# First row tile of q's weights in two transfers, second token half on the other queue, first products in halves

## The chip, the cores and the metric

The kernel runs on one core of one Trainium2 chip. The metric is the device time of one execution in microseconds (us), as the median of several runs. In this kernel TensorE's matmuls are what the profile calls PE, its weight loads PEld; ScalarE is ACT, VectorE DVE, GpSimd POOL, SyncE SP. SP and ACT issue the transfers (DMAs), each on a queue of its own.

## The reference

One layer with two branches on the same 2048 tokens of width 448, mixed by a gate for each token:

```python
x = A_x                                          # (1, 2048, 448)
g = sigmoid((x * gate_w).sum(-1, keepdims=True))
qkv = x @ wqkv                                   # (448, 3*448); 16 heads of 28
# each query looks at 8 keys, its own position and those 2, 4 .. 14 before it
a = (softmax(q . k[pos - 2*w] * 28**-0.5) @ v) @ wo
h = x @ w1 + b1                                  # (448, 1792)
b = relu(h)**2 @ w2 + b2
return g * a + (1 - g) * b
```

All of it is float32.

## The kernel before, in words

Every matrix product is made of three: each operand is split into a high part (a rounded copy, made by ACT or DVE: wqh, x.h, w1h ...) and a low part (the rest, subtracted by DVE: wql, x.l, w1l ...), and PE adds high x high, high x low and low x high in PSUM. A split starts from a raw tile that a transfer brings in from memory (wqraw, xraw).

The 448 rows of a contraction are three row tiles of 128 (k = 0, 1, 2) and one of 64 (k = 3). The tokens are four chunks of 512 (x0 to x3), a chunk four tiles of 128 tokens. For each chunk PE makes q, k and v; then the MLP's h and its output b follow for all chunks, with the attention beside it on POOL and DVE, and the product with wo (a) at the end. q's weights carry two more columns with the gate's weights, so q's products are 450 columns wide, k's and v's 448. The columns are streamed in a woven order: the first of the left half, the first of the right half, the second of the left half, and so on. In the weights' tile the two halves lie apart: 225 columns, one free, 225 columns.

Two things set the order of the work. At the start it is the order in which the code is written: scratch products on zeros (L816, WARM of them, 256 columns each), the first transfers (L819 to L838), and the splits of the first chunk and of q's weights (L839 to L858). Then a planner (class Plan) takes over: it holds a modelled time for PE, starts at START, adds each product's cost, and lets ACT, DVE, POOL and SP issue their jobs in the order in which they would come due. START and FIRST, the modelled length of the first three stretches of products, thus decide where later casts, evacuations and transfers stand.

The first real products are those of qkv_first (L430): four accumulators q[0] to q[3], one for each token tile, in four PSUM banks. For k = 0 it takes the tiles (0, 1), then (2, 3), since the tokens' first half (256 tokens, two tiles) is brought and cast before the second; within a pair the order is high x high, high tokens x low weights, low tokens x high weights. For k = 1 and 2 all four tiles go together. These are the products of L439. From k = 3 on, products of 64 rows run in pairs side by side (L351).

The first transfers: SP issues weights and tokens in turn, 128 rows each; ACT issues the two halves of the first tokens (L823). A transfer's completion is counted on one of eight semaphores that all queues share in turn, so SP's ninth transfer or so waits for the first ones to land. For k = 0 the weights' left half is cast by ACT (L846), the right half by DVE (L847), then DVE casts the tokens' first half (L848) and subtracts the low parts (L850, L854); ACT casts the second half of the tokens (L853).

## Time and profile before

| | before |
|---|---|
| runs (us) | 392.57, 392.83, 392.65; median 392.65 |
| profiled execution: span, first to last instruction | 391.0 us (the page gives its time as this span; the runs' median is 1.65 above it) |
| PE busy | 386.5 us, 99% of the span |
| DVE, POOL, ACT busy | 261.4, 260.6, 205.4 us |
| first scratch product / first real product starts | 0.79 / 5.01 us |
| first product of 64 rows starts | 12.35 us |
| granted TensorE clock over the span | 1.000 |

The profile is one execution. Its page gives the busy time of each engine, the chain of work that ended last, and groups of instructions; its timeline gives rows in the order of time with start and length in us, engine and line, output<-inputs, shape and count, and in brackets how long the engine was idle before and what ended that. A q behind an engine's name is its sequencer, which issues transfers. A matmul's length in a row includes the time until its result has left the array, so rows that follow each other overlap; the distance between starts is the pace.

### The profile page before, as it was taken

The page shows a single profiled execution, that of the slowest core. Times are in us where ns is not written, and L with a number is a line of the kernel's source. Part 1 is how long each engine was busy: PE and PEld are TensorE (multiplying, and loading weights), DVE is VectorE, ACT ScalarE, POOL GpSimd, SP SyncE. Part 2 cuts the span into 40 slices and gives each one's busy share as a digit, 9 for nine tenths or more (in the row PEclk, how much of TensorE's full clock was granted, in tenths as well). Part 3 has the DMA queues.
Part 4 walks back from the last instruction along what each step waited for, and adds up shares of the span by engine and source line. Part 5 has one row for each costly group of instructions (what it writes and reads, how often), then busy time and mean ns, then how long its engine had stood idle before and what let it go on. Part 6 is the DMA issues. An engine that isn't in the chain of part 4 may idle for free.

```text
span 391.0 us, 9273 instructions
## 1 busy us (share of the span) xinstructions
PE 386.5 (99%) x3828; PEld 385.2 (99%) x3828; DVE 261.4 (67%) x348; ACT 205.4 (53%) x501; POOL 260.6 (67%) x165
## 2 busy tenths in 40 slices
PE   9999999999999999999999999999999999999996
PEld 8999999999999999999999999999999999999995
DVE  4525523588685778778656989789666686668454
ACT  4757866362566566445555445345716343456740
POOL 0000002988999989959999887999998979661000
PEclk9999999999999999999999999999999999999999
DMA  7999999997174062654203779655635120226835
GB/s 236 400 355 302 382 376 350 378 370 246 49 246 157 1 219 80 220 171 161 90 2 137 242 183 296 208 124 141 213 111 173 78 96 2 88 63 164 143 107 188
DMA packets 64841, 73.75 MB, mean 189 GB/s; under 512 B 32480, under 2 KB 57632, under 8 KB 64416
## 3 DMA queue, kind: packets, MB, share of 16 engines
q1 hardware_dynamic: 64368, 72.79, 57.2%
q8 instruction: 30, 0.49, 0.5%
q10 hardware_dynamic: 432, 0.38, 0.3%
q14 instruction: 11, 0.09, 0.1%
HBM read 45.71 MB, written 28.25 MB: 189 GB/s over the span
## 4 chain that ended last, share of the span: by engine, by line
PE 99%; DVE 0%; DVEq 0%; issue 0%
PE b L351 33%; PE h L351 32%; PE qkv L351 23%; PE a L351 7%; PE qkv L439 2%; PE warm L817 1%; PE a L1170 1%; DVE bt_b L1053 0%; DVEq L1375 0%
## 5 line engine op out<-in xcount | busy, mean ns | idle before, releaser
L549 POOL TENSOR_TENSOR pp<-q,k 128x896 f32<-128x896 f32 x56 | 116.9, 2124 | 75.1 <-DMA k<-k_d 64.4
L561 POOL TENSOR_TENSOR pp<-lg,v 128x896 f32<-128x896 f32 x64 | 113.8, 1870 | 9.6 <-DVE o L571 5.3
L351 PE MATMUL h<-x,w1h 64*128 64x512 f32 x672 | 116.6, 376 | 0.0
L351 PE MATMUL qkv<-wqh,x 64*128 64x448 f32 (+1 forms) x528 | 82.2, 349 | 0.0
L553 DVE TENSOR_REDUCE lg<-pp 128x32 f32<-128x896 f32 x64 | 66.9, 1076 | 13.9 <-POOL pp L549 13.9
L351 PEld LDWEIGHTS h<-x,w1h 64*128 64x128 f32 x672 | 74.1, 186 | 0.0
L803 DVE TENSOR_TENSOR h<-h,h 128x512 fp32r<-128x512 f32 x56 | 38.6, 690 | 52.4 <-ACT h L802 52.3
L351 PE MATMUL h<-x,w1l 64*128 64x512 f32 x336 | 69.3, 376 | 0.0
L351 PE MATMUL b<-w2bh,h 64*128 64x448 f32 x448 | 67.8, 349 | 0.0
L351 PE MATMUL b<-w2ah,h 64*128 64x448 f32 x448 | 67.6, 349 | 0.0
L571 DVE TENSOR_REDUCE o<-pp 128x112 f32<-128x896 f32 x64 | 67.4, 1064 | 0.0
L351 PEld LDWEIGHTS qkv<-wqh,x 64*128 64x128 f32 x528 | 57.3, 186 | 0.0
L799 ACT ACTIVATE h<-h,b1z 128x512 f32<-128x512 f32 x56 | 36.7, 655 | 36.8 <-PE h L351 36.8
L351 PE MATMUL qkv<-wql,x 64*128 64x448 f32 (+1 forms) x264 | 53.4, 349 | 0.0
L351 PEld LDWEIGHTS b<-w2bh,h 64*128 64x128 f32 x448 | 48.0, 192 | 0.0
L351 PEld LDWEIGHTS b<-w2ah,h 64*128 64x128 f32 x448 | 47.9, 193 | 0.0
L351 PE MATMUL b<-w2al,h 64*128 64x448 f32 x224 | 43.2, 349 | 0.0
L351 PE MATMUL b<-w2bl,h 64*128 64x448 f32 x224 | 43.2, 349 | 0.0
L351 PEld LDWEIGHTS h<-x,w1l 64*128 64x128 f32 x336 | 37.4, 186 | 0.0
L801 ACT ACTIVATE h<-h 128x512 fp32r<-128x512 f32 x56 | 33.4, 597 | 1.5
L373 ACT ACTIVATE st<-qkv 128x448 f32<-128x448 f32 x48 | 24.3, 540 | 17.7 <-PE qkv L351 12.9
L802 ACT ACTIVATE h<-h 128x512 f32<-128x512 f32 x56 | 33.1, 592 | 0.0
(111 smaller groups left out, 547.7 us busy)
## 6 DMA issues: line engine op xcount, KB each, us to landing
v<-v_d SPq DMA_DIRECT2D x8, 840.0 KB, 6.0
x_d<-x SPq DMA_DIRECT2D x12, 512.0 KB, 7.3
x<-x_d SPq DMA_DIRECT2D x12, 512.0 KB, 3.5
k<-k_d SPq DMA_DIRECT2D x7, 840.0 KB, 6.5
q_d<-st SPq DMA_DIRECT2D x8, 448.0 KB, 6.1
k_d<-st SPq DMA_DIRECT2D x8, 448.0 KB, 5.8
v_d<-st SPq DMA_DIRECT2D x8, 448.0 KB, 6.2
o_d<-o SPq DMA_DIRECT2D x16, 224.0 KB, 2.2
```

The costliest lines, as they stand in the source:

```text
L351: nc.tensor.matmul(woven_out(acc.pt, acc.n), a[rows], woven(w[rows]), start=acc.todo == acc.all, stop=acc.todo == 1)
L373: nc.scalar.activation(st[0][:, :, t % 2].rearrange("p (i g) c -> p i g c", i=2), unwoven(pt[:, :D]).rearrange("p i (g c) -> p i g c", c=C ...
L439: nc.tensor.matmul(woven_out(acc.pt, NQ), a, woven(w), start=k == j == 0, stop=False)
L549: nc.gpsimd.tensor_mul(pr.rearrange("p (w c) -> p w c", w=W), q[:, s:s + 1].to_broadcast([P, W, C]), k[:, s:s + W])
L553: nc.vector.tensor_reduce(lgs[i][:, s], pr.rearrange("p (w h d) -> p w h d", w=W, h=HG), axis=AX.X, op=ALU.add)
L561: nc.gpsimd.tensor_mul(pr.rearrange("p (h d w) -> p w h d", h=HG, w=W), lgs[i][:, s][:, :, :, None].to_broadcast([P, W, HG, DH]), vs[i][:, ...
L571: nc.vector.tensor_reduce(o_t[par, s][:, g * C:(g + 1) * C], pr.rearrange("p (c w) -> p c w", w=W), axis=AX.X, op=ALU.add)
L799: a = add(ACT, 656.0, lambda pt=pt, r=r: nc.scalar.activation(pt, pt, AF.Relu, bias=b1t[:, f + r:f + r + 1]), ready, *bias_job[:2], prio=NEXT)
L801: b = add(ACT, 600.0, lambda pt=pt, hh=hh: nc.scalar.activation(hh, pt, AF.Square), a, prio=NEXT)
L802: a = add(ACT, 600.0, lambda pt=pt: nc.scalar.activation(pt, pt, AF.Square), b, prio=NEXT)
L803: low = add(DVE, 690.0, lambda pt=pt, hh=hh, hl=hl: nc.vector.tensor_sub(hl, pt, f32(hh)), a, prio=NEXT)
L817: nc.tensor.matmul(warm[:, :2 * P].rearrange("p (i n) -> p i n", i=2), zero, zeros, start=True, stop=True)
```

## The change

q's weights of row tile 0 come in two transfers of 225 columns, both on SP's queue. The second half of the first tokens moves from ACT's queue to SP's, behind them. Both weight halves are cast by ACT, one after the other, and DVE casts only the tokens. The first two products of high x high, tiles 0 and 1, are made in two halves each, with one scratch product of 128 columns between the halves. For that the columns of q's accumulators are laid out in two slots of 226 (in each the 225 columns woven by halves, one of them twice), so that all of q's products of the first chunk have 452 columns; the evacuation and the gate's column read that layout. The scratch products at the start are 15 of 256 columns and one of 128 in place of 18. START falls from 4850 to 4300.

```diff
--- before.py
+++ after.py
@@ -33,9 +33,9 @@
 MM448, MM512 = 189.2, 216.0
 PE_LAT = 175.0
 LAT = 60.0
-START = 4850.0
+START = 4300.0
 ORDER = (3, 0, 1, 2)
-WARM = 18
+WARM = 15
 FIRST = (2700.0, 2350.0, 2300.0)
 PP_BUFS = 4
 ST_BUFS = 3
@@ -206,6 +206,23 @@
     def woven_out(pt, n):
         return (pt[:, :2 * NH] if n == NQ else pt[:, :n]).rearrange("p (n i) -> p n i", i=2)
 
+    HS = NH // 2 + 1
+
+    def in_slots(w, part=None):
+
+        n, o = (2, 0) if part is None else (1, part * NG)
+        return bass.AP(tensor=w.tensor, offset=w[:, o:o + 1].offset, ap=[list(w.ap)[0], [NG, n], [1, HS], [D // 4, 2]])
+
+    def slots_out(pt, part=None):
+        n, o = (2, 0) if part is None else (1, part * 2 * HS)
+        return pt[:, o:o + n * 2 * HS].rearrange("p (s n i) -> p s n i", s=n, i=2)
+
+    def product(acc, a, w, part=None, **kw):
+        if acc.slots:
+            nc.tensor.matmul(slots_out(acc.pt, part), a, in_slots(w, part), **kw)
+        else:
+            nc.tensor.matmul(woven_out(acc.pt, acc.n), a, woven(w), **kw)
+
     def unwoven(t):
         return t.rearrange("p (n i) -> p i n", i=2)
 
@@ -333,7 +350,7 @@
         def __init__(self, tag, name, n, todo=None, now=True):
             self.ring, self.n, self.tag, self.name = rings[tag], n, tag, name
             self.all = self.todo = todo or 21
-            self.rows, self.after = None, tuple(self.ring.take())
+            self.rows, self.after, self.slots = None, tuple(self.ring.take()), False
             if now:
                 need(*self.after)
                 self.open()
@@ -348,7 +365,7 @@
             for r, (acc, a, w, *_) in enumerate(pair):
                 rows = slice(r * 64, r * 64 + 64)
                 assert acc.rows in (None, r)
-                nc.tensor.matmul(woven_out(acc.pt, acc.n), a[rows], woven(w[rows]), start=acc.todo == acc.all, stop=acc.todo == 1)
+                product(acc, a[rows], w[rows], start=acc.todo == acc.all, stop=acc.todo == 1)
                 acc.todo, acc.rows, acc.after = acc.todo - 1, r, ()
             plan.pe(MM512 if pair[0][0].n == CH else MM448 + (pair[0][0].n - D) * 1.7)
 
@@ -370,13 +387,18 @@
         def evacuate():
             if first:
                 st[0] = xap.tile([P, G, 2, C], F32, tag="stage", name=f"st{c}_{tl}_{b}", bufs=ST_BUFS)
+            if acc.slots:
+                nc.scalar.activation(st[0][:, :, t % 2].rearrange("p (s i) c -> p s i c", i=2),
+                                     slots_out(pt).rearrange("p s n i -> p s i n")[:, :, :, :C], AF.Copy)
+                return
             nc.scalar.activation(st[0][:, :, t % 2].rearrange("p (i g) c -> p i g c", i=2),
                                  unwoven(pt[:, :D]).rearrange("p i (g c) -> p i g c", c=C), AF.Copy)
 
         jobs = [add(ACT, 540.0, evacuate, ready, *st[1], *st[2], prio=SOON)]
         st[2].append(jobs[0])
         if b == 0:
-            jobs.append(add(ACT, 165.0, lambda: nc.scalar.activation(zt[:, par, t:t + 1], pt[:, D + 1:D + 2], AF.Copy),
+            z = 4 * HS - 1 if acc.slots else D + 1
+            jobs.append(add(ACT, 165.0, lambda: nc.scalar.activation(zt[:, par, t:t + 1], pt[:, z:z + 1], AF.Copy),
                             jobs[0], prio=SOON))
             z_jobs[par].append(jobs[1])
         acc.ring.give(*jobs)
@@ -430,13 +452,18 @@
     def qkv_first(x):
         four = range(4)
         q = accs(0, 0, four, "bbbb")
+        for acc in q:
+            acc.slots = True
         for k in range(3):
             todo = [full(x, q[i], i, 0, (k,)) for i in four]
             for some in ((0, 1), (2, 3)) if k == 0 else (four,):
                 for j in range(3):
-                    for i in some:
-                        acc, a, w, *_ = todo[i][j]
-                        nc.tensor.matmul(woven_out(acc.pt, NQ), a, woven(w), start=k == j == 0, stop=False)
+                    for part in (0, 1) if k == j == 0 and some == (0, 1) else (None,):
+                        for i in some:
+                            acc, a, w, *_ = todo[i][j]
+                            product(acc, a, w, part, start=k == j == 0 and part != 1, stop=False)
+                        if part == 0:
+                            keep_busy(1)
             plan.pe(FIRST[k])
         for acc in q:
             acc.todo = 3
@@ -813,22 +840,26 @@
     zeros = nc.const_aps.tensor(0.0, [P, 2, P], F32).bitcast(F32R)
     nc.vector.memset(none, 0.0)
 
-    for _ in range(WARM):
-        nc.tensor.matmul(warm[:, :2 * P].rearrange("p (i n) -> p i n", i=2), zero, zeros, start=True, stop=True)
+    def keep_busy(n):
+        nc.tensor.matmul(warm[:, :n * P].rearrange("p (i n) -> p i n", i=n), zero, zeros[:, :n], start=True, stop=True)
+
+    for i in range(WARM):
+        keep_busy(2)
+    keep_busy(1)
 
     raws = [rawp.tile([P, 4, 512], F32, tag="raw", name="wqraw0")]
     rx = rawp.tile([P, 4, 512], F32, tag="raw", name="xraw0")
     halves = slice(0, 256), slice(256, CH)
-    for cols in halves:
-        nc.scalar.dma_start(rx[:, 0, cols], xT[0, :, 0, cols])
+    nc.scalar.dma_start(rx[:, 0, halves[0]], xT[0, :, 0, halves[0]])
     for k in range(4):
         if k < 3:
-            nc.sync.dma_start(raws[0][:, k, :NQ], wqkv[0, :, k])
+            for cols in (slice(0, NH), slice(NH, NQ)) if k == 0 else (slice(0, NQ),):
+                nc.sync.dma_start(raws[0][:, k, cols], wqkv[0, :, k, cols])
         else:
             for b, rows in ((0, slice(0, 64)), (1, slice(64, P))):
                 nc.sync.dma_start(raws[0][rows, k, :NQ], wqkv[b, rows, k])
-        if k:
-            nc.sync.dma_start(rx[:, k], xT[0, :, k])
+        cols = slice(0, CH) if k else halves[1]
+        nc.sync.dma_start(rx[:, k, cols], xT[0, :, k, cols])
     for b, tag in ((1, "k"), (2, "v")):
         raw = attp.tile([P, 3, D], F32, tag=tag, name=f"wqraw{b}")
         for k in range(3):
@@ -843,10 +874,10 @@
             nc.scalar.activation(wh, raw, AF.Copy)
             nc.vector.tensor_sub(wl, raw, f32(wh))
         else:
-            nc.scalar.activation(wh[:, 0], raw[:, 0], AF.Copy)
-            nc.vector.tensor_copy(wh[:, 1], raw[:, 1])
             nc.vector.tensor_copy(x.h[0][:, halves[0]], rx[:, 0, halves[0]])
-            for i in (1, 0):
+            for i in range(2):
+                nc.scalar.activation(wh[:, i], raw[:, i], AF.Copy)
+            for i in range(2):
                 nc.vector.tensor_sub(wl[:, i], raw[:, i], f32(wh[:, i]))
         for n, cols in enumerate(halves if k == 0 else (slice(0, CH),)):
             if k or n:
```

What stands where. PE at its start (qkv_0_0 is the accumulator of q's tile 0, qkv_1_0 that of tile 1; wqh and wql are the high and low weights, x_0 the first chunk's row tile 0). Before:

```order
L817 MATMUL warm<-const-float32-0.0 128x256 x18
L439 MATMUL qkv_0_0_195<-wqh,x_0_171 128x450
L439 MATMUL qkv_1_0_196<-wqh,x_0_171 128x450
L439 MATMUL qkv_0_0_195<-wql,x_0_171 128x450
L439 MATMUL qkv_1_0_196<-wql,x_0_171 128x450
L439 MATMUL qkv_0_0_195<-wqh,x_0_171 128x450
L439 MATMUL qkv_1_0_196<-wqh,x_0_171 128x450
```

After:

```order
L844 MATMUL warm<-const-float32-0.0 128x256 x15
L844 MATMUL warm<-const-float32-0.0 128x128
L222 MATMUL qkv_0_0_194<-wqh,x_0_170 128x226
L222 MATMUL qkv_1_0_195<-wqh,x_0_170 128x226
L844 MATMUL warm<-const-float32-0.0 128x128
L222 MATMUL qkv_0_0_194<-wqh,x_0_170 128x226
L222 MATMUL qkv_1_0_195<-wqh,x_0_170 128x226
L222 MATMUL qkv_0_0_194<-wql,x_0_170 128x452
L222 MATMUL qkv_1_0_195<-wql,x_0_170 128x452
L222 MATMUL qkv_0_0_194<-wqh,x_0_170 128x452
L222 MATMUL qkv_1_0_195<-wqh,x_0_170 128x452
```

The two products of high weights and high tokens became four of half the width around one scratch product; behind them nothing changed places.

SP's queue at the start (wqraw: q's raw weights; xraw: the first chunk's raw tokens). Before, with ACT issuing both token halves at the same time on its own queue:

```order
L826 DMA wqraw_149<-wqkv 128x450 x2
L831 DMA xraw_150<-xT 128x512
L826 DMA wqraw_149<-wqkv 128x450
L831 DMA xraw_150<-xT 128x512
L829 DMA wqraw_149<-wqkv 64x450 x2
L831 DMA xraw_150<-xT 128x512
```

After, with only the first token half on ACT's queue:

```order
L857 DMA wqraw_147<-wqkv 128x225 x2
L862 DMA xraw_148<-xT 128x256
L857 DMA wqraw_147<-wqkv 128x450
L862 DMA xraw_148<-xT 128x512
L857 DMA wqraw_147<-wqkv 128x450
L862 DMA xraw_148<-xT 128x512
L860 DMA wqraw_147<-wqkv 64x450 x2
L862 DMA xraw_148<-xT 128x512
```

One weight transfer became two, the token half stands third, and each later transfer of this group has one issue more ahead of it.

SP's queue a little later, where the planner sets the order (xraw: the next two chunks' tokens; early: raw weights of the MLP; q_d, k_d: stores of q and k from the staging buffers st). Before:

```order
L663 DMA xraw_236<-xT 128x2048
L663 DMA xraw_238<-xT 128x2048
L388 DMA q_d<-st_0_0_287 128x4x224
L388 DMA q_d<-st_2_0_295 128x4x224
L673 DMA early<-w 128x1792
L388 DMA k_d<-st_0_1_383 128x4x224
L388 DMA k_d<-st_2_1_407 128x4x224
```

After:

```order
L690 DMA xraw_238<-xT 128x2048
L690 DMA xraw_248<-xT 128x2048
L700 DMA early<-w 128x1792
L410 DMA q_d<-st_0_0_294 128x4x224
L410 DMA q_d<-st_2_0_303 128x4x224
L410 DMA k_d<-st_0_1_385 128x4x224
L913 DMA x_d<-x_0_170 128x1024
```

The load of early moved ahead of the two stores of q, and one store of k behind the first stores of tokens (x_d).

## The prediction

> **What bounds the kernel now.** I read the page's busy shares and its chain first, then PE's waits, the chain in order of time, and last the first eight microseconds instruction by instruction. From the page, busy time of each engine and the chain's shares:
>
> ```profile
> PE 386.5 (99%) x3828; PEld 385.2 (99%) x3828; DVE 261.4 (67%) x348; ACT 205.4 (53%) x501; POOL 260.6 (67%) x165
> ...
> PE 99%; DVE 0%; DVEq 0%; issue 0%
> ```
>
> The waits of PE (engine, line, what it waited for: total us, times, longest), and the first rows of the chain in order of time (start, length, what):
>
> ```profile
> engine line waited for: us in total, times, longest us
> PE warm L817 <- PEq L1372: 0.8, 1, 0.8
> ```
>
> ```profile
> 0.79 4.18 PE warm L817 x18
> 5.01 7.41 PE qkv L439 x36
> 12.42 86.58 PE qkv L351 x909
> ```
>
> PE waits once, for the launch, and its 386.5 us fill the span from 0.79 on. From 5.01 product follows product to the end. So the time is the moment at which the first real products are through, plus work that the change leaves almost as it is. Only stretch 0.79 to about 12.4 can give anything.
>
> The timeline of PE, asked for in narrow windows, one row for each product where its pace matters (start, length, line, out<-in, shape, count; a row of several has the count behind the x):
>
> ```profile
> 0.79 0.77 PE L817 MATMUL warm<-const-float32-0.0 128*128 128x256 f32 x2 [0.79 <-PEq L1372]
> ...
> 4.55 0.42 PE L817 MATMUL warm<-const-float32-0.0 128*128 128x256 f32 x1
> ...
> 5.01 0.71 PE L439 MATMUL qkv<-wqh,x 128*128 128x450 f32 x1
> ...
> 5.51 0.45 PE L439 MATMUL qkv<-wqh,x 128*128 128x450 f32 x1
> ...
> 5.79 0.35 PE L439 MATMUL qkv<-wql,x 128*128 128x450 f32 x1
> ...
> 6.17 0.92 PE L439 MATMUL qkv<-wqh,x 128*128 128x450 f32 x4
> ...
> 7.32 1.30 PE L439 MATMUL qkv<-wqh,x 128*128 128x450 f32 x6
> ...
> 9.21 1.68 PE L439 MATMUL qkv<-wqh,x 128*128 128x450 f32 x8
> 10.73 0.92 PE L439 MATMUL qkv<-wql,x 128*128 128x450 f32 x4
> ```
>
> Scratch product 2 starts at 1.14 (0.79 + 0.77 - 0.42) and the 18th at 4.55: 0.213 us each for 256 columns, 0.83 ns a column. Eight products from 9.21 to 10.73 take 0.19 each, 0.42 ns a column. So PE starts at half pace. The first real product takes 0.50 (5.01 to 5.51): 450 columns at 0.83 are 0.375, so 0.13 is the restart after idling. The second takes 0.28, between 0.375 and 0.19: half of it ran slow, so PE sped up at about 5.69.
>
> Who lets it start? The timeline of all engines, same columns (a bracket has the idle time before and who ended it):
>
> ```profile
> 0.75 0.86 SPq L826 DMA_DIRECT2D wqraw<-wqkv  x2
> 0.75 0.89 ACTq L823 DMA_DIRECT2D xraw<-xT  x2
> ...
> 1.65 0.43 SPq L831 DMA_DIRECT2D xraw<-xT  x1
> ...
> 4.38 0.39 ACT L846 ACTIVATE wqh<-wqraw 128x225 fp32r<-128x225 f32 x1 [1.43 <-DMA wqraw<-wqkv]
> 4.38 0.28 DVE L847 CAST wqh<-wqraw 128x225 fp32r<-128x225 f32 x1 [3.52 <-DMA wqraw<-wqkv]
> 4.57 0.28 DVE L848 CAST x<-xraw 128x256 fp32r<-128x256 f32 x1
> 4.77 0.69 DVE L850 TENSOR_TENSOR wql<-wqraw,wqh 128x225 fp32r<-128x225 f32 x2
> 4.97 0.50 PEld L439 LDWEIGHTS qkv<-wqh,x 128*128 128x128 f32 x2 [0.30 <-ACT wqh L846]
> ...
> 5.38 0.42 DVE L854 TENSOR_TENSOR x<-xraw,x 128x256 fp32r<-128x256 f32 x1
> ...
> 5.68 0.42 ACT L853 ACTIVATE x<-xraw 128x256 fp32r<-128x256 f32 x1 [0.91 <-DMA xraw<-xT]
> ...
> 6.47 0.61 ACT L853 ACTIVATE x<-xraw 128x512 fp32r<-128x512 f32 x1
> ```
>
> The bracket names ACT, but ACT is done at 4.77; DVE's cast of the tokens ends at 4.85, and the product starts 0.16 later. That cast started at 4.57, right behind the weight cast. So the first product stands 0.44 behind the start of the token cast.
>
> **The change, part by part.** What the first transfers cost, from the DMA view of narrow windows: issue rows (KB, us to landing), then packets of 1.75 to 4.5 us by queue (q1 is SP's, q10 ACT's; share of 16 engines) and the total of 4.5 to 5.7:
>
> ```profile
> wqraw<-wqkv SPq DMA_DIRECT2D x1, 225.0 KB, 3.6
> ...
> xraw<-xT ACTq DMA_DIRECT2D x1, 128.0 KB, 4.5
> ```
>
> ```profile
> DMA packets 486, 0.65 MB, mean 236 GB/s; under 512 B 39, under 2 KB 485, under 8 KB 486
> ...
> q1 hardware_dynamic: 269, 0.44, 57.6%
> q10 hardware_dynamic: 217, 0.20, 24.3%
> ```
>
> ```profile
> DMA packets 273, 0.41 MB, mean 341 GB/s; under 512 B 39, under 2 KB 149, under 8 KB 273
> ```
>
> *Weights in two transfers.* 57.6% of 16 x 2.75 us over 269 packets is 94 ns for a weight row of 1.8 KB; 24.3% over 217 is 49 ns for 1 KB of tokens. Each of 16 engines serves eight of either before the first tokens are in: 1.14 us. Rows of 0.9 KB cost at most what 1 KB does, so it becomes 0.78: the weights' first half and the first tokens land 0.36 earlier. Ends: 0 (if the last engine is late by its start, not by its bytes) and 0.44 (all that follows the cast); I take 0.36, since the two queues fill 82% of the engines' time there. The price is 128 packets more, 8 on an engine: at most 0.39 for the second weight half, which then lands near 4.4, as the whole does now (0.75 + 3.6).
>
> *Token half behind them on SP's queue.* It is issued at 1.65 in place of 1.19, and all that SP issues behind it comes two issues of 0.46 later for the weights and tokens of rows 128 to 383. Their bytes are the same in sum, and 0.65 MB have moved by 4.5 where 0.98 MB are wanted before row tile 1's tokens are in: the queue is full well before, so they land as now, about 6.35 (cast at 6.47). Bounds: unmoved, or 0.94 late with the issue. The cover is PE's own work: their cast ends at 7.08 and is used at 7.70 (third of the row at 7.32); an earlier PE eats 0.1 of these 0.6, a transfer 0.94 late would cost 0.4. The half itself was cast at 5.68 and used at 6.55; it lands earlier now, with no second queue beside it. The Trainium skill, DMA: Bandwidth & Descriptors, Issuing engines are not separate DMA queues, says that a second issuing engine saves only issue time: by that rule moving the half costs no bandwidth. The trace agrees as far as 341 GB/s with almost one queue is not below 236 with two.
>
> *DVE's weight cast goes to ACT.* DVE's token cast no longer stands behind it: 4.21. ACT's first half: landed at 4.0, cast 4.02 to 4.41, in time. Second half: 4.4 to 4.8, wanted at 5.26; DVE's two low parts then end by about 5.25, wanted at 5.64. ACT was idle 0.91 there.
>
> *Half products and scratch.* First product at 4.21 + 0.44 = 4.65. Still at half pace: 0.13 restart, 226 columns at 0.83 = 0.19 each: two to 5.16, the scratch product of 128 columns (0.11) to 5.26, two more to 5.64. Then the low parts, for which PE was ready at 5.79 before; 0.05 of theirs still runs slow and loses 0.025. Gain 0.125. The trace has no product under 256 columns; bounds for a half are its columns (0.19) and a whole product's time (0.375); I take the columns, since 256 and 450 columns cost by the column. Scratch products before: 15 of 0.213 and one of 0.11, ending at 4.23, hidden in the wait.
>
> *Two columns more.* 44 products of 452 for 450 columns (32 whole here, 12 in the row tile behind): 44 x 0.84 ns = 0.04, on the path. The token product's evacuation by ACT reads the same 448 columns in another order: nothing, as ACT waits for PE between.
>
> Sum: 0.125 - 0.04 = 0.09 off 391.0, so 390.9. The median of the runs, 392.65, lies 1.65 above that span; with it **392.55 us**.
>
> **The rivals.**
>
> *The clock rises later* (the other side). PE sped up 4.9 us after its first product, with one idle spell of 0.25 (4.76 to 5.01). Now it idles from 4.23 to 4.65, or to 5.0 if the tokens don't land earlier. If that spell starts the count anew, the rise comes 4.9 us after 4.65, at 9.55: 3.9 us at half pace cost 1.9, and the time is 394.5. It decides (over 393.44) from a rise 1.8 us later on. For: the idle spell grows by two thirds or threefold. Against: 0.25 did not do it, and four half products with a scratch product fill the rest. The Trainium skill, TensorE: Matmul & The Clock Gate, Part 1, has a free-running window of about 3.4 us that must be busy before the clock rises; by that rule a spoilt window costs 3.4 us at half pace, an estimate of 1.7, and the time would be 394.25. The trace agrees as far as 4.9 us lie between one window and two.
>
> *Nothing lands earlier.* The first product stays at 5.01, the halves and the scratch run slow to 5.69 (0.55 of their 0.86 after the restart) and the rest at full pace to 5.85: 0.06 lost, with the columns 0.10: 392.75. For: landing comes 3.6 us after issue for 225 KB, which at 341 GB/s are 0.7; the rest is delay that smaller rows may not shorten. Against: the 82%.
>
> *The whole 0.36 to 0.44 is kept*, if the clock in the timed runs rises before the first product: 392.25 to 392.35. For: one execution shows one rise, and nothing in it ties that moment to the kernel's start. Against: the rise at 5.69 is all there is to go by.
>
> *Half products cost as much as whole ones.* Four at 0.375 slow: 4.65 + 0.13, then 0.91 slow of 1.61, the rest 0.35: 6.04, 0.25 lost, 392.95; were they dearer still, it goes on to slower. For: no such row. Against: cost by the column at 256 and 450.
>
> *A store is late.* With the planner's new start, SP issues the 896 KB of early weights before the stores of q, no longer after:
>
> ```profile
> 16.29 1.61 SPq L388 DMA_DIRECT2D q_d<-st  x2
> 17.95 1.01 SPq L673 DMA_DIRECT2D early<-w  x1
> ...
> q_d<-st SPq DMA_DIRECT2D x2, 448.0 KB, 5.4
> early<-w SPq DMA_DIRECT2D x1, 896.0 KB, 7.7
> ...
> 21.81 1.42 ACT L373 ACTIVATE st<-qkv 128x448 f32<-128x448 f32 x3 [0.56 <-PE qkv L351]
> ...
> 26.28 0.26 ACT L358 ACTIVATE qkv<-b1z 1x1 f32<-1x1 f32 x2 [2.01 <-PE qkv L351]
> ```
>
> At 341 GB/s these are 2.7 us, so the store lands near 24.4, not 21.7; ACT's third evacuation waits for its buffer, and behind it stands the small ACT write of 26.28, for which PE waits. With a weight cast that now stands between, ACT is free near 25.6, 0.6 before that write's turn. Were the store 1.6 us later still, PE would stop for 1 at most: 393.55.
>
> **How the numbers follow.** Chances: the forecast 0.50; nothing lands earlier 0.18; the whole shift kept 0.14; halves dear 0.08 (half of it beyond 393.44); clock late 0.06; store late 0.02; unforeseen gain 0.02. Forecast and its two neighbours hold 0.82. The range is 392.15 to 393.0: the lower end is the whole shift less 0.1 for the runs' spread (392.57 to 392.83), the upper one halves as dear as whole products. Of what would be told from no change, 0.2% or 0.79 us (below 391.86, above 393.44): faster 0.02, slower 0.04 + 0.06 + 0.02 = 0.12, same 0.86.
>
> **What would show it.** Right: first half product near 4.65 with DVE's token cast near 4.2, the whole low products from about 5.65, row tile 1 (the x6 row's third) near 7.6, the pair rows near 12.25, no second wait of PE. Wrong: a token cast at 4.57, half products further apart than 0.19, products still 0.375 apart behind 6, or PE waiting for ACT's cast of row tile 1's tokens or near 27.

## The result and the profile after

The changed kernel takes 394.30 us (median of 16 runs, 393.56 to 396.19) against 392.98 for the kernel before on the same chip (16 runs, 392.57 to 394.04): the ratio is 1.0031, 95% interval 1.0023 to 1.0040. That is slower by 1.3 us; the forecast was 392.55, its range ended at 393.0.

The profiled execution took 393.94 us, its span is 392.1 (before 391.0). From its page, busy times and the chain's shares; then PE's waits and two pieces of the chain:

```profile
PE 386.3 (99%) x3829; PEld 384.6 (98%) x3829; DVE 258.0 (66%) x347; ACT 206.3 (53%) x502; POOL 262.6 (67%) x165
...
PE 97%; DMA 1%; SPq 0%; ACT 0%; DVE 0%; DVEq 0%; issue 0%
```

```profile
PE warm L844 <- PEq L1403: 0.8, 1, 0.8
PE qkv L222 <- DVE x L877: 0.5, 1, 0.5
PE qkv L222 <- ACT x L884: 0.2, 1, 0.2
```

```profile
2.60 4.74 DMA xraw<-xT
8.05 5.27 PE qkv L222 x25
```

PE is as busy as before. But it waits twice more, and a transfer is now part of the chain: row tile 1's tokens, issued at 2.60 and landed at 7.34. The timeline of the start:

```profile
4.51 0.29 DVE L877 CAST x<-xraw 128x256 fp32r<-128x256 f32 x1 [3.65 <-DMA xraw<-xT]
...
4.95 0.45 PE L222 MATMUL qkv<-wqh,x 128*128 128x226 f32 x2 [0.53 <-DVE x L877]
...
6.76 0.58 ACT L874 ACTIVATE wqh<-wqraw 128x450 fp32r<-128x450 f32 x1 [1.19 <-DMA wqraw<-wqkv]
...
7.37 0.63 ACT L884 ACTIVATE x<-xraw 128x512 fp32r<-128x512 f32 x1
...
8.05 0.84 PE L222 MATMUL qkv<-wqh,x 128*128 128x452 f32 x3 [0.22 <-ACT x L884]
```

Two issues more, not one, stand ahead of row tile 1 on SP's queue: its tokens were issued at 1.65 before. Its weights are cast at 6.76 (before 6.01), its tokens at 7.37 (6.47), and the row tile's first product stands at 8.05 (7.70). The first product of 64 rows marks the end of the start. Before and after:

```profile
12.35 0.46 PE L351 MATMUL qkv<-w7h,x 64*128 64x450 f32 x2
```

```profile
12.86 0.46 PE L222 MATMUL qkv<-w7h,x 64*128 64x452 f32 x1
```

So the start lost 0.51: 0.35 up to row tile 1's first product, the rest in PE's restart behind that wait (0.11) and in the wider products. From here PE's last product ends 374.93 us later before and 374.96 after: nothing else is lost while PE works. The rest is behind it. Last product and last store, before and then after:

```profile
386.93 0.35 PE L1170 MATMUL a<-woh,o 128*128 128x448 f32 x1
...
388.15 0.33 SPq L1061 DMA_DIRECT2D out<-bt_b  x1
```

```profile
387.46 0.35 PE L1201 MATMUL a<-woh,o 128*128 128x448 f32 x1
...
388.69 0.33 SPq L1092 DMA_DIRECT2D out<-bt_b  x1
```

Before, the span ends at 391.0, 3.72 us behind PE's end (387.28); after, at 392.1, 4.33 behind it (387.82), though the last store is issued 0.88 behind PE's end in both. The sum is 0.51 + 0.03 + 0.61 = 1.15, where the spans lie 1.14 apart. In the trace's semaphore instructions, which these views leave out, SP at the end waits for the eight completion counters in a fixed order, in six waits. The last store has landed 2.58 after PE's end in both kernels. Before, the last two stores are counted on the last two counters of that order, and SP is through 2.60 after PE's end. One transfer more in the kernel shifts the last store to the counter of the third wait: SP stands there for 1.23, has three waits left and is through at 2.80. Then one of its closing instructions comes 0.34 after the one ahead of it instead of 0.05.

### The profile page after: what moved, and what is told of

The parts are those of the page before. It is cut to its first block, busy times and chain, and to the rows that moved or that the text cites. A ratio compares the mean times of both kernels' runs of the same rounds, so it can differ in the third digit from the quotient of the medians.

```text
span 392.1 us, 9279 instructions
## 1 busy us (share of the span) xinstructions
PE 386.3 (99%) x3829; PEld 384.6 (98%) x3829; DVE 258.0 (66%) x347; ACT 206.3 (53%) x502; POOL 262.6 (67%) x165
## 4 chain that ended last, share of the span: by engine, by line
PE 97%; DMA 1%; SPq 0%; ACT 0%; DVE 0%; DVEq 0%; issue 0%
PE b L224 32%; PE h L224 32%; PE qkv L224 23%; PE a L224 7%; PE qkv L222 1%; DMA xraw<-xT 1%; PE a L1201 1%; SPq L857 0%; ACT x L884 0%; DVE bt_b L1084 0%; SPq L862 0%; DVEq L1406 0%
## 5 line engine op out<-in xcount | busy, mean ns | idle before, releaser
L224 PE MATMUL h<-x,w1h 64*128 64x512 f32 x672 | 121.3, 376 | 0.0
L224 PEld LDWEIGHTS h<-x,w1h 64*128 64x128 f32 x672 | 80.0, 186 | 0.0
L224 PE MATMUL h<-x,w1l 64*128 64x512 f32 x336 | 73.8, 376 | 0.0
L224 PEld LDWEIGHTS qkv<-wqh,x 64*128 64x128 f32 x528 | 60.8, 186 | 0.0
L224 PE MATMUL qkv<-wql,x 64*128 64x448 f32 (+1 forms) x264 | 56.6, 349 | 0.0
L224 PEld LDWEIGHTS b<-w2bh,h 64*128 64x128 f32 x448 | 51.5, 192 | 0.0
L224 PEld LDWEIGHTS b<-w2ah,h 64*128 64x128 f32 x448 | 51.4, 193 | 0.0
L224 PE MATMUL b<-w2bl,h 64*128 64x448 f32 x224 | 46.2, 349 | 0.0
L224 PEld LDWEIGHTS h<-x,w1l 64*128 64x128 f32 x336 | 41.9, 186 | 0.0
L224 PEld LDWEIGHTS qkv<-wql,x 64*128 64x128 f32 x264 | 33.0, 186 | 0.0
```

The lines of the kernel that those rows point to most:

```text
L224: nc.tensor.matmul(woven_out(acc.pt, acc.n), a, woven(w), **kw)
```

## The experiments

All medians stand beside runs of the kernel before on the same chip, whose medians were 392.7 to 393.2. "Start" is the first product of 64 rows in the one profile of each, "end" the time from PE's last product to the end of the span.

| kernel | median (us) | ratio, 95% interval | start | end |
|---|---|---|---|---|
| changed | 394.30 | 1.0023 to 1.0040 | 12.86 | 4.33 |
| half back on ACT's queue | 393.60 | 1.0008 to 1.0035 | 13.37 | 3.92 |
| before + half on SP's queue | 393.78 | 1.0006 to 1.0035 | 12.56 | 3.72 |
| before + weights in two | 393.90 | 1.0025 to 1.0053 | 13.00 | 3.94 |
| changed, products whole | 394.47 | 1.0025 to 1.0049 | 13.59 | 4.33 |
| row tile 1 issued as before | 395.10 | 1.0030 to 1.0062 | 13.02 | 3.88 |
| before + two 4-byte-row transfers early | 393.78 | 1.0012 to 1.0034 | 12.94 | 4.39 |
| changed, START 4850 | 394.86 | 1.0035 to 1.0080 | 13.64 | 4.35 |
| changed, 18 + 1 scratch products | 394.45 | 1.0024 to 1.0054 | 13.38 | 4.33 |
| before, 15 scratch products | 394.20 | 1.0002 to 1.0033 | 12.27 | 3.73 |
| before, 21 scratch products | 392.96 | 0.9991 to 1.0008 | 12.45 | 3.74 |
| changed, row tile 1 on ACT's queue | 394.63 | 1.0029 to 1.0060 | 13.41 | 3.90 |
| the same, products whole | 394.02 | 1.0019 to 1.0044 | 12.70 | 3.88 |
| changed, right weights on ACT's queue | 393.95 | 1.0029 to 1.0065 | 12.99 | 3.94 |
| the same, products whole, 20 + 1 scratch | 393.83 | 1.0018 to 1.0042 | 13.19 | 3.92 |
| before + two 4-byte-row transfers late | 393.90 | 1.0018 to 1.0038 | 12.17 | 4.41 |
| changed, bias in one transfer | 394.63 | 1.0031 to 1.0054 | 13.82 | 3.71 |

**The parts apart.** Two theories at first: late issue (row tile 1 stands two issues further back) and short rows (128 more packets).

```diff
# half back on ACT's queue
-    nc.scalar.dma_start(rx[:, 0, halves[0]], xT[0, :, 0, halves[0]])
+    for cols in halves:
+        nc.scalar.dma_start(rx[:, 0, cols], xT[0, :, 0, cols])
...
-        cols = slice(0, CH) if k else halves[1]
-        nc.sync.dma_start(rx[:, k, cols], xT[0, :, k, cols])
+        if k:
+            nc.sync.dma_start(rx[:, k], xT[0, :, k])
```

> The changed kernel with the second token half back on ACT's queue (weights still in two transfers, products still in halves). Late issue (the half on SP's queue pushes row tile 1's weights and tokens 0.94 us back): only the second weight transfer is now ahead of them, so they are issued near 1.65 and 2.13 instead of 2.13 and 2.60; the cast of row tile 1's tokens starts near 6.9 instead of 7.37, the first product of 64 rows near 12.4, and the time is some 0.5 us below the changed kernel's 394.3, about 393.8. Short rows (128 more packets slow the engines, whichever queue carries the half): that cast stays near 7.4, the time near 394.3.

> The kernel before with one thing changed: the second token half is issued by SP behind q's first weights instead of by ACT. Late issue: everything behind it on SP's queue is issued 0.47 later; row tile 1's tokens are cast near 6.95 instead of 6.47, end near 7.55 with 7.70 as the moment of their use, so PE loses 0 to 0.2 and the time is 393.0 to 393.2. If one queue alone also carries less than two, the cast comes at 7.3 or later and the time is 393.4 or more. Short rows: no short row is added, the time is 393.0 and the cast stays at 6.47.

> The kernel before with one thing changed: row tile 0 of q's weights comes in two transfers of 225 columns on SP's queue. Late issue: as for the half, 0.47 later for all behind it, cast of row tile 1's tokens near 6.95, time 393.0 to 393.2. Short rows: 8 more packets on each engine, of which each costs up to 0.06 us (0.63 mean of the changed kernel against half of 94 ns), so that cast comes near 7.3 and the time near 393.5. In neither does the first product move from 5.01, if the last landing of the first tokens stays at 4.5.

The second and third are the kernel before with that line of the change's diff alone. (0.63 there is a slip for 0.063.) Each part alone costs, 0.7 and 0.8 by the medians, and with the half taken back the median falls by 0.7. So neither alone is innocent, but by which path each costs is not told. The second has three of its twelve times at 395.13 to 395.68 and the others at 394.07 or less, the third five at 395.27 to 395.62 and the others at 393.93 or less; both profiles are from the lower part. And in the profiles of the first and the third PE waits ahead of row tile 1: in the first the tokens were cast at 3.85, but the second weight half landed only at 5.74, and PE waited for it for 1.3; in the third that half landed at 5.11, DVE cast it ahead of the tokens, and PE's first product stands at 5.83.

> The changed kernel with the first products whole, 450 columns in the old layout, without the scratch product between (transfers, casts, the sixteen scratch products and the planner's start as changed). If the transfers are what costs, row tile 1's tokens are still cast near 7.4 and the time stays near 394.3 (less 0.04 for the columns). If the halves, the scratch product or the layout cost, the time falls by 0.5 or more, towards 393.6.

In `qkv_first` the slots and the halves were taken out. The time stays, with an end of 4.33 as in the changed kernel: halves, scratch product and columns are not the loss.

**Issue or rows, in the kernel.**

```diff
# row tile 1 issued as before
     nc.scalar.dma_start(rx[:, 0, halves[0]], xT[0, :, 0, halves[0]])
+    nc.scalar.dma_start(raws[0][:, 0, NH:NQ], wqkv[0, :, 0, NH:NQ])
+    nc.scalar.dma_start(rx[:, 0, halves[1]], xT[0, :, 0, halves[1]])
... (SP leaves both out)
# two 4-byte-row transfers early (kernel before, behind q's first weights)
+            for i in range(2 if k == 0 else 0):
+                nc.sync.dma_start(spare[:, i:i + 1], xT[0, :, 0, i:i + 1])
... (spare is a tile that nothing reads)
```

> The changed kernel with the same three short transfers shared out otherwise: SP issues the first weight half and right behind it row tile 1's weights and tokens (issued at 1.19 and 1.65, as in the kernel before), ACT issues the first token half, the second weight half and the second token half. Late issue: row tile 1's tokens are cast near 6.5 again and the time falls to about 393.1 to 393.3. Short rows: as many short rows stand before row tile 1 as in the changed kernel, so its tokens are still cast near 7.4 and the time stays near 394.3.

> The kernel before with two transfers of 128 rows of 4 bytes (into a tile that nothing reads) between q's first weights and row tile 1 on SP's queue: two issues more, almost no bytes, all wide rows as before. Late issue: row tile 1's tokens are issued 0.9 later and cast near 7.3, the first product of 64 rows stands near 12.8, and the time is 393.5 to 394. Short rows: 512 bytes cost the engines nothing to speak of, the tokens are cast near 6.5 and the time is 393.0 to 393.2.

In the first, row tile 1's tokens landed at 6.35, exactly as before, behind all the short rows. The time missed. In its profile (393.65, the fastest of eight times) PE does not wait for row tile 1, but 0.3 for the second weight half, which ACT's queue brought at 5.24. Five of the eight times lie between 395.08 and 395.90, and what those wait for is not seen. In the second two issues with almost no bytes cost 1.0, of which 0.67 is the end, told below. Its row tile 1 tokens are issued at 2.60, as in the changed kernel, yet they land at 6.87, not at 7.34, and PE does not wait for them. The start of its profile is late by something else: the first tokens landed at 4.83 (before 4.52), and the granted clock was full only from 6.58 (before from 5.69).

> The changed kernel with the planner's start of the kernel before (4850), so that the order of stores and loads from 10 us on is like that of before; the first 10 us stay as changed. If the first transfers carry the loss, 394.3 as the changed kernel; if the planner's order carries a part of it (no wait of PE behind 13 us speaks for that), up to 0.5 less.

> The changed kernel with 18 scratch products of 256 columns ahead of the one of 128, so that PE is busy until about 4.87 instead of 4.23. In the six profiles so far PE's pace doubled at different moments (before 4.6 in one, at 5.7 and 6.2 in others). If idling from 4.23 on puts that off in part of the runs, the median falls by 0.3 or more, to 394.0 or less, and the slowest runs go. If not, it stays at 394.3 or rises by up to 0.2, since the first real product waits for scratch products in those runs where its tokens land early.

Neither the planner's start nor more scratch products gain anything in the changed kernel. But the changed kernels agree in their wait. With products whole, with START 4850 and with 18 + 1 scratch products PE waits for ACT's cast of row tile 1's tokens:

```profile
PE qkv L224 <- ACT x L882: 1.7, 1, 1.7
```

```profile
PE qkv L222 <- ACT x L884: 0.8, 1, 0.8
```

```profile
PE qkv L222 <- ACT x L884: 1.1, 1, 1.1
```

Their row tile 1 tokens landed at 8.13, 8.12 and 7.87.

**The transfers alone.** To get around the scatter, a kernel made the first transfers eight times in each of seven forms, another again with other forms. Of those that the texts below do not spell out, two is the form before with the weights in two transfers, and dots is the form before with two transfers of 4-byte rows ahead of row tile 1.

> The first transfers by themselves, eight times each in seven forms in turn, nothing else in the kernel (all of the computation is left out, the output is zeros). A form starts when the one ahead of it has landed whole; each transfer has a tile of its own, named by its form, so the list of transfers gives the median from issue to landing. Late issue: in the changed form and in the one with two transfers of 4-byte rows (dots), row tile 1's tokens (tone) land as long after their issue as in the form before or sooner, and later in all only by the 0.94 of two more issues; in the form shared (row tile 1 issued as before, short rows on ACT's queue) they land as before. Short rows: they land about 0.9 us later than before from the start of the form in all forms with weights in two transfers (after, two, shared), and as before in the form with the half alone on SP's queue (half) and in dots. First tokens (tleft): 0.36 us sooner with the short weight transfer, if the prediction's sum of rows was right.

> The first transfers by themselves again (all of the computation left out, zeros as output), seven forms in turn, eight times each: before, after and half as in the first such run; halfdot (half with a transfer of 4-byte rows behind the first weights, so that row tile 1 is issued as late as after, with wide rows only); rows (after, but the weights' two transfers are 64 whole rows each); swap (after, with the second token half behind row tile 1); right (after, with the second weight half on ACT's queue). Late issue: halfdot and rows land row tile 1's tokens as late as after, about 1.1 behind before; swap and right land them 0.45 sooner than after. Short rows: halfdot and rows land them like half, 0.4 to 0.5 behind before, and right as late as after, or at most 0.2 sooner.

From the list of transfers of the second (tile, queue, count, KB, median us from issue to landing; other rows left out):

```profile
before_tone<-xT SPq DMA_DIRECT2D x8, 256.0 KB, 4.8
after_tone<-xT SPq DMA_DIRECT2D x8, 256.0 KB, 4.7
half_tone<-xT SPq DMA_DIRECT2D x8, 256.0 KB, 4.6
halfdot_tone<-xT SPq DMA_DIRECT2D x8, 256.0 KB, 4.8
...
swap_tone<-xT SPq DMA_DIRECT2D x8, 256.0 KB, 4.4
right_tone<-xT SPq DMA_DIRECT2D x8, 256.0 KB, 4.3
...
before_tleft<-xT ACTq DMA_DIRECT2D x8, 128.0 KB, 3.4
after_tleft<-xT ACTq DMA_DIRECT2D x8, 128.0 KB, 2.7
half_tleft<-xT ACTq DMA_DIRECT2D x8, 128.0 KB, 3.6
```

From the list of the first:

```profile
two_tone<-xT SPq DMA_DIRECT2D x8, 256.0 KB, 4.4
...
dots_tone<-xT SPq DMA_DIRECT2D x8, 256.0 KB, 4.3
```

Issue to landing of row tile 1's tokens is 4.8 before and 4.7 after; what differs is the issue, 0.95 and 1.90 into the form. Counted from the form's start they land (medians of eight) at 5.83 before, 6.71 after, 6.00 in half, 6.67 in halfdot, 6.34 in rows, 5.86 in swap, 5.84 in right; in the first such kernel before and after were 5.66 and 6.75, two 5.83, shared 5.73, dots 6.20. halfdot has no short row and is as late as after; shared and right have all short rows and land like before. Short rows are out. And the first tokens land 0.66 sooner after, not 0.36; but with the weights in two alone 0.06 sooner (3.31 for 3.37).

Late issue is a part of the loss, not the whole. dots issues row tile 1's tokens as late as after (1.92), with almost no bytes more on the queue, and they land 0.54 behind before, where after is 1.09 behind. One issue more costs next to nothing in right and swap, 0.17 in two, 0.17 and 0.40 in half; rows issues them at 2.39, later than after, and lands them sooner. What makes the other part is open. A lower rate stands beside it: between 3.0 and 5.5 us of a form the engines moved 214 to 254 GB/s in the four forms of the second kernel with seven transfers on SP's queue, 316 to 325 in those with five or six. But swap, at 214, is one of the four and lands row tile 1 like before, with the second token half behind it. The kernel itself shows the lower rate too, from 4.5 to 7 us of its span; before, after, and with the right weights on ACT's queue:

```profile
DMA packets 568, 0.91 MB, mean 363 GB/s; under 512 B 74, under 2 KB 318, under 8 KB 568
```

```profile
DMA packets 392, 0.66 MB, mean 266 GB/s; under 512 B 41, under 2 KB 244, under 8 KB 392
```

```profile
DMA packets 566, 0.92 MB, mean 368 GB/s; under 512 B 68, under 2 KB 348, under 8 KB 566
```

In the five profiles with the changed list of first transfers these 2.5 us move 0.61 to 0.72 MB, in the four with the list of before 0.89 to 0.92. Why seven transfers on one queue slow the engines is open.

**Row tile 1 back in time, two ways.**

```diff
# row tile 1 on ACT's queue; SP leaves it out
+    nc.scalar.dma_start(raws[0][:, 1, :NQ], wqkv[0, :, 1])
+    nc.scalar.dma_start(rx[:, 1], xT[0, :, 1])
...
# right weights on ACT's queue; SP leaves them out
+    nc.scalar.dma_start(raws[0][:, 0, NH:NQ], wqkv[0, :, 0, NH:NQ])
...
```

> The changed kernel with row tile 1's weights and tokens issued by ACT right behind the first token half (at 1.19 and 1.65, as in the kernel before), the other first transfers on SP as changed. Nothing else moves, and the second token half keeps its place, unlike in the run with the short transfers shared out. Late issue: row tile 1's tokens land near 6.4 to 6.7 instead of 7.3 to 8.1, PE waits for them for 0.3 at most, the first product of 64 rows stands near 12.2 to 12.5 and the time is 392.5 to 393.2. If something else than their issue made them late (the queue that carries them, the number of rows ahead), they still land behind 7.3 and the time stays near 394.3.

> The same with the first products whole (450 columns, no scratch product between) and 17 scratch products of 256 columns and one of 128 at the start (PE busy until 4.66). Late issue: 392.5 to 393.2, as the halves and columns are worth 0.1; with the longer warm-up the runs should not fall into two groups 1.6 us apart as those of the kernel before with 15 scratch products did.

> The changed kernel with one transfer moved: the second weight half is issued by ACT behind the first token half, so SP issues the second token half at 1.19, row tile 1's weights and tokens at 1.65 and 2.13 (the changed kernel 2.13 and 2.60). Late issue: row tile 1's tokens land near 6.6 instead of 7.3 to 8.1, the first product of 64 rows stands near 12.2 to 12.6, and the time is 392.6 to 393.4. If the loss is elsewhere, the time stays near 394.3 with the tokens on time.

> The same transfers with whole first products of 450 columns and 20 scratch products of 256 columns and one of 128, so that PE is busy until 5.3 at half pace (less where the pace doubles sooner). Late issue and idle spell together: no run 1.5 us above the others, 392.6 to 393.2, as the kernel before. If only the row tile counted, as the run beside it.

All four missed. Row tile 1's tokens landed at 7.19, 6.51, 7.03 and 6.86. The first two issue them at 1.67, and the kernel before, where they land at 6.35, at 1.65: a landing in one profile does not follow its issue alone. And something else was last. In the first it is the second token half (landed at 6.96, in the changed kernel at 5.13), in the other three the second weight half (5.15, 5.36 and 5.63; in the form right it landed 4.17 into the form, which would be 4.9 here). PE's wait in the second, then in the third with its cause on ACT:

```profile
PE qkv L224 <- ACT wqh L880: 0.9, 1, 0.9
```

```profile
PE qkv L222 <- ACT wqh L880: 0.7, 1, 0.7
```

```profile
5.39 0.39 ACT L880 ACTIVATE wqh<-wqraw 128x225 fp32r<-128x225 f32 x1 [1.40 <-DMA wqraw<-wqkv]
```

The engines serve 0.98 MB up to row tile 1's last row; in these four profiles another of its pieces came last and was waited for. No version of the first transfers beats the kernel before.

**The clock.** The kernel before with other numbers of scratch products (WARM):

> The kernel before with 15 scratch products instead of 18: PE idles from 4.12 to about 5.0 instead of from 4.76. If that spell puts off the doubling of PE's pace in part of the runs, these runs are 1.5 to 1.8 us longer and stand apart from the others, and the median rises by 0.2 or more. If it does not, the median stays at 392.8 to 393.1 with the spread of the kernel before.

> The kernel before with 21 scratch products, so that PE idles nowhere ahead of its first real product, which at half pace comes at 5.4 to 5.5 instead of 5.0. If the idle spell puts off the doubling of the pace in part of the runs, there is no run 1.5 us above the fast ones, and the median stays within 0.2 of before (0.4 us later at half pace costs up to 0.2). If the spell has nothing to do with it, the spread stays as it is and the median rises by up to 0.4.

With 15, the twelve times fall into two groups, five of 392.63 to 393.05 and seven of 394.18 to 394.96, whose medians lie 1.74 apart; with 21 all lie between 392.54 and 393.60. So a longer idle spell ahead of the first product makes part of the executions longer. That PE's full pace comes later in these is argued from the size alone: the granted clock is full for 385.71 us in thirteen of the kernels' profiles and for 389.12 in five, 3.41 more, and 3.41 us at half pace cost 1.7, an estimate from these two figures. The kernel before with the weights in two, where PE waited 0.9 for its first product, shows the same: seven of its twelve times are 393.49 to 393.93, five 395.27 to 395.62. No profile fell into the later group, so the late rise itself was not seen. Nor does the spell explain all such times: the kernel before with the half on SP's queue has three apart, and in its profile PE waits for nothing but the launch. PE's first products in two executions, of before with 15 scratch products and of before with the two early transfers:

```profile
5.00 0.62 PE L439 MATMUL qkv<-wqh,x 128*128 128x450 f32 x2 [0.69 <-DVE x L848]
```

```profile
5.30 1.09 PE L439 MATMUL qkv<-wqh,x 128*128 128x450 f32 x2 [0.34 <-DVE x L851]
```

The same two products are through in 0.62 in one execution, where the granted clock is full from 4.81, and in 1.09 in the other, where it is full from 6.58. Over the profiles the rise came between 4.1 and 6.6, not always at 5.7.

**The end.**

```diff
# two 4-byte-row transfers late (kernel before)
     def mlp_one():
+        for i in range(2):
+            nc.sync.dma_start(spare[:, i:i + 1], xT[0, :, 0, i:i + 1])
...
# bias in one transfer (changed kernel)
-    bj = [dma(... b1t[:, :NFA], b1[:, :NFA] ...), dma(... b1t[:, NFA:], b1[:, NFA:] ...),
+    bj = [dma(lambda: nc.sync.dma_start(b1t, b1), 128, 56, prio=LAST, at=60000.0),
...
```

> The kernel before with two transfers of 128 rows of 4 bytes (into a tile that nothing reads) on SP's queue near 100 us, where SP is idle; the start is untouched. End: SP's closing waits take the completion counters in a fixed order, and two transfers more shift the last stores to counters that come earlier in it; from PE's end to the end of the span 4.3 to 4.4 instead of 3.72, the first product of 64 rows near 12.4, and the time 0.5 to 0.7 above before, 393.4 to 393.6. Start only (all of the loss is late first transfers): the same as before, 392.7 to 393.1.

> The changed kernel with the two loads of the MLP's first bias (3.5 KB each, near 60 us) made one, so that the number of transfers is that of before; the start is as changed. End: 3.7 from PE's end to the end of the span, the time 0.4 to 0.6 below the changed kernel, 393.7 to 393.9; what then is left above 392.9 is the start's. Start only: 394.3 as the changed kernel.

The first shows the end by itself. Its start is the earliest of all, the last store is issued 0.88 behind PE's end as ever, and the span of 391.5 ends 4.41 behind PE:

```profile
12.17 0.46 PE L351 MATMUL qkv<-w7h,x 64*128 64x450 f32 x2
```

```profile
386.75 0.35 PE L1173 MATMUL a<-woh,o 128*128 128x448 f32 x1
...
387.98 0.33 SPq L1064 DMA_DIRECT2D out<-bt_b  x1
```

It measures 0.9 above before, 0.2 more than the 0.69 of its end. The second has its end back at 3.71 as expected, but the time missed: its start fell at 13.82, the latest of all, and PE waits once more, for a reload of tokens:

```profile
PE qkv L222 <- ACT x L884: 1.8, 1, 1.8
PE warm L844 <- PEq L1402: 0.8, 1, 0.8
PE h L224 <- DMA x<-x_d: 0.3, 1, 0.3
```

So that the end's share can be won back is not shown. Over all profiles the end goes with two counts: 3.71 to 3.74 with as many transfers as before, 3.88 to 3.94 with one more, 4.33 to 4.41 with one or two more and two instructions more on SP's queue. What delays SP's closing instruction in the last of these was not tried apart.

## Why the prediction was wrong, point by point

*The step that failed is "they land as now, about 6.35".* It argued that SP's queue is full well before and that bytes, not issues, set the landing of row tile 1's tokens. With the same bytes they land 0.9 to 1.1 later by themselves. In the five kernels with the changed list they land at 7.34 to 8.30, and PE waits for them in all five, for 0.2 to 1.8; with the list of before they land at 6.06 to 6.58 and PE never waits for them. About half of the delay (0.54) came with two issues that bring almost no bytes. The other half came only with the token half's bytes on SP's queue, where the rate was lower; what makes it is open. The bound that the text named and set aside, 0.94 late at a cost of 0.4, is what came in the profiled execution: 0.99 late, and 0.51 lost. By the medians, 1.32 less 0.61 for the end leaves 0.7. The five profiled starts with that list are 1.15 later in the mean than the four with the list of before (13.46 against 12.31): executions scatter by more than the sum's terms.

*The end was no term of the sum.* It was taken to move with PE. 0.61 of the loss is there, more than any term of the sum. The 1.65 that was put on it for the runs joined one execution's span to the median of three: in the profiled executions that have both on record the time stands 1.78 to 1.86 above the span, and over 16 runs the kernel before takes 392.98.

*First tokens 0.36 sooner.* Right in sign, too small, and not by the sum of rows that it was worked out from. In the transfers alone the whole change gives 0.66 and 0.64, but the weights in two, which is all that the sum counts, 0.06 (in the one profile with nothing else changed the tokens landed at 3.83 for 4.52). Four of the five profiles cast them at 3.85 to 3.90. The profiled execution of the changed kernel is the fifth (4.51), hence its 4.95 for the first half product, not 4.65. The earlier cast gained nothing, since the slack that was to hide row tile 1's landing is spent by that much earlier: with tokens cast at 3.85, PE waited 1.8 for the next row tile.

*"By that rule moving the half costs no bandwidth."* The Trainium skill, DMA: Bandwidth & Descriptors, Issuing engines are not separate DMA queues, says that a second issuing engine saves only issue time. Here the issue time counted, and the rate fell as well, from 363 to 266 GB/s. The 341 of the trace was read at a moment when ACT's queue still carried the second half (it landed at 5.66).

*DVE's weight cast* was not what the token cast stood behind: the tokens' own last landing, 4.52, was.

*Halves, scratch, two columns:* right (34, not 32, of the first 36 products stay whole, which is worth under 0.01). Whole products change nothing that can be told, and PE's time from the first product of 64 rows to its last grew by 0.03.

*Clock later (0.06).* Its 394.5 and 394.25 are close to the 394.30 that came, but that is chance. In the profiled execution the granted clock is full from 4.93, before from 5.69; in the other four profiles with the changed list from 4.05, 4.46, 4.63 and 6.35, at times of 394.46 to 394.82. The changed kernel's times show no two groups, only one run at 396.19, and three scratch products more don't help it. What the rival describes may be what parts the kernel before with 15 scratch products, whose later group has its median at 394.45. The 1.74 between its groups agrees with the free-running window of the Trainium skill, TensorE: Matmul & The Clock Gate, Part 1: 3.4 us at half pace are 1.7, an estimate.

*Nothing lands earlier (0.18)* is what the profiled execution shows for the first tokens (4.49 for 4.52), but not the other four. *Halves dear, store late:* not seen; PE has no wait near 27, and the planner's old start gains nothing. Of the signs that the text named for being wrong, PE's wait for ACT's cast of row tile 1's tokens came.

## What to carry to other kernels

A transfer put ahead of others on a queue can delay all of them, even where the bytes are the same; here by nothing to 0.4 us for one issue more, and by 0.5 to 1.1 for two. Ask of each one behind it how much slack its landing has, and take away from that slack what the change itself brings forward. A landing in one profile is the last of many engines and scatters by a microsecond; make the transfers by themselves a few times in each order and take the medians. Look at the end of the span too: a transfer more or less anywhere can move it.

## What the hardware showed that was not expected

- The closing waits of SP make the end depend on how many transfers the kernel has: two transfers near 100 us that nothing reads moved it from 3.72 to 4.41.
- Most rows of 900 bytes took 42 ns, of 1 KB 46 and of 1.8 KB 75, but single ones at the changed kernel's start up to 1.0 us; the prediction's 94 ns for 1.8 KB and 49 ns for 1 KB were means over such stalls.
- Seven transfers on one queue at the start moved a quarter less than five there and two on the other (0.66 against 0.91 MB in 2.5 us).
- PE's pace doubled 3.3 to 5.8 us after its first scratch product, at another moment in each execution.
